# A long convolution and an MLP on one core: where the stores of batch 0's second stage are issued

## The chip, the cores and the metric

The kernel runs on one core of one Trainium2 chip. The metric is the device time of one execution in microseconds (us); what is compared is the median of several executions. The engines go by short names: PE is TensorE (PEld its weight loads), ACT is ScalarE, DVE is VectorE, POOL is GpSimd and SP is SyncE, which does no arithmetic and issues DMAs. All DMAs of the core are carried out by the same 16 DMA engines.

## The reference

A long convolution over 12480 positions is computed for two batches by Fourier transforms, multiplied by its input, and sent through an MLP. Cut to what matters (all arrays are float32):

```python
h_filt = (np.maximum(pos_emb @ w1, 0.0) @ w2) * window        # the filter
u = x * v                                                     # (2, 12480, 128)
Uf = np.fft.rfft(u, n=L, axis=1)                              # L = 2 * 12480
Hf = np.fft.rfft(h_filt, n=L, axis=0)
y = np.fft.irfft(Uf * Hf[None, :, :], n=L, axis=1)[:, :S, :]
attn = x * y
h = attn.reshape(B * S, D) @ w_in                             # 128 -> 2048
out = np.maximum(0.01 * h, h) @ w_out                         # 2048 -> 128
```

## The kernel before, in words

The transform of length 98 x 128 is done in steps of matrix products, with scratch arrays in DRAM between the steps. In time the kernel has three parts.

*First stage (to about 150 us).* The first transform step for batch 0 and for the filter. SP alone issues every DMA, loads and stores, among them the stores of the result `o` to the scratch array `scr1`.

*Second stage of batch 0 (about 150 to 320 us).* This is what the change touches. The work is cut into 25 chunks (`NCH`), taken in the order `ORD`, which begins with the chunks 13 to 24 and ends with 10 and 11. The loop `for i, c in enumerate(ORD)` runs over them. For each chunk

- `load_b` (line 705) brings a tile `bin`, 768 KB, from `scr1`; it is issued three chunks ahead, and there are four such tiles;
- `hidden` (line 790) puts the filter's part of the *next* chunk through PE (`ep`), and ACT copies it to `es` (line 793);
- PE makes the filter spectrum `hp` (line 846), ACT copies it to `hs` (line 850, two tiles `hs`), and `store_h` stores it to `hspec` with two DMAs of 256 KB (line 815): batch 1 reads it much later;
- PE makes the spectrum `up` (line 135); DVE and POOL multiply it by `hs` (`product`, lines 143 and 144) into `pin`; `up` has only one pair of PSUM tiles, so PE starts the next chunk's `up` when DVE has read this one;
- PE transforms back (`back_halves`, line 163, `dp`) the chunk *before*; `evac` copies it with ACT to `ct` (line 238, two tiles `ct`), and `store_back` stores it to `scr2` with one DMA of 512 KB (line 220);
- between these, a generator `weights` is advanced five steps a chunk. It loads a piece of the MLP's weights (lines 717 and 718, 256 KB each, every third chunk, eight pieces in all), and DVE, ACT and PE turn it into two parts each (lines 80 to 91, 732 to 762).

Late in the loop SP also begins the loads that the third part needs: `upper_c` and `rows_c` read `scr2` into `cin` (lines 629 to 650), `fetch_a` brings some 1.4 MB for batch 1 (lines 249, 67 and 69, twice), `load_gx` more (lines 609 to 620), and for the last two chunks `last_c` copies a few rows from `ct` straight into `cin` (line 657). The first MLP tile waits for the last of these.

*The MLP (from about 325 us to the end)* runs on PE, and batch 1's convolution is worked in between.

The order of the work is written out by hand: each engine takes its instructions in the order of the program, and one that waits holds all behind it on its engine. For DMAs this goes for the queue of the engine that issues them. In this stage the loads are issued by SP, and the stores of `hs` and of `ct` by ACT, between its copies. Each DMA also takes one of eight completion semaphores in turn (`DMAHW0` to `DMAHW7` in the rows below), which SP and ACT share; before it is issued it waits until the DMA that had that semaphore before has landed.

The kernel before has a list `late` in this loop that is always empty; a `flush` that empties it is called in the third part only.

Of the kernel before, what the change touches and what calls it, by code (L numbers as in the profile page):

```python
# [30 lines left out]
def tile_conv_mlp(ctx, tc, x, v, pos_emb, w1, w2, w_in, w_out, cf, cr, cg, cb, ci, cw, out):  # L31
    nc = tc.nc
# [77 lines left out]
    def run(g):  # L110
        for _ in g:
            pass
# [14 lines left out]
    def chunk(c):  # L127
        k0 = c * KC
        return k0, min(KC, NA - k0)
# [88 lines left out]
    def store_back(b, c, ct, eng):  # L218
        k0, n = chunk(c)
        eng.dma_start(out=scr2[b][k0:k0 + n].rearrange("k r m e -> (r m) k e"),  # L220
                          in_=ct[:, :n].rearrange("p k s d -> p k (s d)"))
# [13 lines left out]
    def back_evac(dp, ct, n):  # L235

        for s in range(2):
            nc.scalar.copy(ct[:, :n, s, :], dp[s][:, :n * D].rearrange("p (k d) -> p k d", d=D))
            yield


    with tc.manual_schedule():
# [17 lines left out]
        def mult_a(c):  # L260
            ft, (xt, vt) = got.pop(c)
            nc.gpsimd.tensor_tensor(out=xt, in0=xt, in1=vt, op=ALU.mult)
            u1[c] = ft, xt

        with ExitStack() as st:
# [89 lines left out]
            late = []  # L355
            for c in range(NC0):
# [23 lines left out]
                late = []  # L380
# [224 lines left out]
        def load_gx(t):  # L605
            b, mp = divmod(t, NT)
            g = gring()
            for r in range(2):
                nc.sync.dma_start(out=g[KH * r:KH * r + KH, :4 * NA],
                                  in_=cg[:KH, mp, r].rearrange("k p m a -> k (p m a)"))  # L610
            xt = xring()
            ms = slice(2 * mp, 2 * mp + 2)
            full = x[b, :(NA - 2) * NB, :].rearrange("(i w p n) d -> w i p n d", w=2, p=2, n=HB)
            for w in range(2):
                nc.sync.dma_start(out=xt[64 * w:64 * w + KH - 1], in_=full[w, :, :, ms, :])
            r0 = (NA - 2) * NB
            nc.sync.dma_start(out=xt[KH - 1:KH],
                              in_=x[b, r0:r0 + NB, :].rearrange("(o p n) d -> o p n d", o=1, p=2)[:, :, ms, :])
            r0 += NB + 2 * mp
            nc.sync.dma_start(out=xt[GAP - 1:GAP, 0], in_=x[b, None, r0:r0 + 2, :])  # L620
            ld[t] = (g, xt)
# [21 lines left out]
        def rows_c(t, j, lo, hi):  # L643

            b, mp = divmod(t, NT)
            ci_t = cin[t]
            ms = slice(2 * mp, 2 * mp + 2)
            ks = slice(KH * j + lo, KH * j + hi)
            for r in range(2):
                nc.sync.dma_start(out=ci_t[KH * r + lo:KH * r + hi, j].rearrange("k m s d -> k (m s d)"),  # L650
                                  in_=scr2[b][ks, r, ms, :].rearrange("k m e -> k (m e)"))

        def last_c(ct, k0, n, engs):

            for m in range(2):
                for r in range(2):
                    engs[2 * m + r].dma_start(out=cin[0][KH * r + k0:KH * r + k0 + n, 0, m],
                                      in_=ct[HB * r + m:HB * r + m + 1, :n])
# [38 lines left out]
        with ExitStack() as st:  # L697
# [4 lines left out]
            def load_b(c):  # L702
                k0, n = chunk(c)
                t = sbb.tile([128, KC, 2, C0], F32, tag="bin", name="bin", bufs=4)
                nc.sync.dma_start(out=t[:, :n].rearrange("p k s e -> p k (s e)"), in_=scr1[:, k0:k0 + n, :])
                bins[c] = t
# [61 lines left out]
            late = []  # L768
            turn = [0]

            def two(tag):
                return [psb.tile([128, 512], F32, tag=tag, name=tag + "p", bufs=2) for _ in range(2)]
# [6 lines left out]
            def ahead(n):  # L779
                for _ in range(4 * n):  # L780
                    next(conv)

            def hidden(c):

                n, t = chunk(c)[1], bins[c]
                ep = psb.tile([128, 2, 2, 2, 64], F32, tag="e", name="ep")
                for s in range(2):
                    for k in range(n):
                        i = 64 * (k % 2)
                        nc.tensor.matmul(ep[i:i + 64, k // 2, :, s, :], t[:, k, s, :FO], mb[:, s],  # L790
                                         start=True, stop=True)
                eh[c] = sbb.tile([128, 2, 2, 128], F32, tag="es", name="es")
                nc.scalar.copy(eh[c][:, :n // 2], ep[:, :n // 2].rearrange("p j r s q -> p j r (s q)"))

            def evac(c):
                ct = sbb.tile([128, KC, 2, D], F32, tag="ct", name="ct", bufs=2)
                k0, n = chunk(c)
                end = c == ORD[-1]
                dp = dps.pop(c)
                if end:  # L800
                    for s, copy in ((0, nc.scalar.copy), (1, nc.vector.tensor_copy)):
                        copy(ct[:, :n, s, :], dp[s][:, :n * D].rearrange("p (k d) -> p k d", d=D))
                else:
                    run(back_evac(dp, ct, n))
                if c in ORD[-2:]:
                    last_c(ct, k0, n, [nc.sync] * 3 + [nc.scalar if end else nc.sync])
                store_back(0, c, ct, nc.sync if end else nc.scalar)

            def store_h(c, hs, i):

                w = chunk(c)[1] * D

                def put(eng):
                    for s in range(2):
                        eng.dma_start(out=hspec[c][:, :, s, :w], in_=hs[HB * s:HB * s + HB, :, :w])
                put(nc.scalar)

            eh, dps = {}, {}
            first_c = upper_c(0)
# [1 line left out]
            next(conv)  # L821
            hidden(ORD[0])
            for i, c in enumerate(ORD):
                if i + 3 < NCH:
                    load_b(ORD[i + 3])
                if NCH - 10 <= i < NCH - 5:
                    next(first_c)
                if i == NCH - 2:
                    load_gx(0)
                if i == NCH - 1:  # L830
                    load_gx(1)
                    rows_c(0, 0, 0, (MID - 2) * KC)
                if i in FETCH:
                    fetch_a(FETCH.index(i))
                if i == NCH - 2:
                    mult_a(0)
                for f in late:
                    f()
                late = []
                n = chunk(c)[1]  # L840
                t, es = bins.pop(c), eh.pop(c)
                hp = two("h")
                for ri in range(2):
                    for k in range(n):
                        h, j = 64 * (k % 2), ri * n // 2 + k // 2
                        nc.tensor.matmul(hp[k % 2][:, D * j:D * j + D], es[h:h + 64, k // 2, ri, :], w22[h:h + 64, :],
                                         start=True, stop=True)
                hs = sbb.tile([128, 2, KC // 2, 2, D], F32, tag="hs", name="hs", bufs=2)
                for k in range(2):
                    nc.scalar.copy(hs[:, :, :n // 2, k, :],  # L850
                                   hp[k][:, :n * D].rearrange("p (r j d) -> p r j d", r=2, d=D))
                hs = hs.rearrange("p r j i d -> p r (j i d)")
                up = two("u")
                fwd(up, lambda s: t[:, :n, s, FO:], n)
                if i + 1 < NCH:
                    hidden(ORD[i + 1])
                store_h(c, hs, i)
                for _ in range(3):
                    next(wprep, None)
                pins[c] = sbb.tile([128, 2, 512], F32, tag="pin", name="pin", bufs=2)  # L860
                ab = [sbb.tile([128, 2, 512], F32, tag=g, name=g) for g in ("ta", "tb")]
                product(ab, up, hs, n * D, pins[c], nc.vector if i >= NCH - 2 else nc.gpsimd)
                if i >= 1:
                    b4 = ORD[i - 1]
                    dps[b4] = two("d")
                    back_halves(dps[b4], pins.pop(b4), b4)
                    evac(b4)
                for _ in range(2):
                    next(wprep, None)

            def flush():
                for f in late:
                    f()
                late.clear()

            ahead(1)
            run(wprep)
            mult_a(1)
            dps[ORD[-1]] = two("d")
            back_halves(dps[ORD[-1]], pins.pop(ORD[-1]), ORD[-1])  # L880
            evac(ORD[-1])
            run(join_hi(0))
            run(upper_c(1))
# [433 lines left out]
```

## Time and profile before

| | us |
|---|---|
| median of 3 executions | 1598.55 (1595.64 to 1606.63) |
| the profiled execution, its own time | 1601.6 |
| its span in the trace | 1599.7 |
| PE busy in the span | 1555.3 (97%) |
| DVE busy | 1138.7 (71%) |
| ACT busy | 998.1 (62%) |

The profile is of one execution. Its span runs from the first to the last instruction; the 1.9 us between span and time lie around it. Times in the rows below count from the span's start. A DMA-issuing instruction (engine names with a q: SPq, ACTq) is not counted as busy time of its engine, though it takes that engine's turn.

### The profile page before, as it was taken

To read this page: it belongs to the slowest core of one execution; us is meant where nothing else is said; L and a number is where in the kernel's file an instruction comes from. 1 tells how busy PE (TensorE), PEld (TensorE's weight loads), DVE (VectorE), ACT (ScalarE), POOL (GpSimd) and SP (SyncE) were. 2 spreads that over 40 slices of the span, in tenths; PEclk is the share of its full clock that TensorE was granted. 3 is DMA by queue.
4 is the path that set the end of the run, shared out by engine and by line. 5 is a ranking of instruction groups with operands and counts; after the bars stand their busy time and mean duration, and the time that the engine had idled before them with its cause. 6 is when DMAs were issued, how large, how long until landed. Compare 5 with 4: busy or idle time off the path is not lost.

```text
span 1599.7 us, 27485 instructions
## 1 busy us (share of the span) xinstructions
PE 1555.3 (97%) x9241; PEld 1322.6 (83%) x9241; DVE 1138.7 (71%) x1785; ACT 998.1 (62%) x2108; POOL 767.0 (48%) x806
## 2 busy tenths in 40 slices
PE   7888999899999999999999999999999999999998
PEld 7887555588889888888888888988888888888888
DVE  6874888756975566666676765677777777777776
ACT  2332555346664477777777776667777676777776
POOL 6772122146654275867776873633443433334310
PEclk9999999999999999999999999999999999999999
DMA  9998999767767477657556650421212212121200
GB/s 268 304 307 283 320 318 340 243 198 203 222 198 216 136 194 192 197 162 197 173 160 181 171 153 32 138 85 55 69 54 68 80 57 89 56 61 59 64 11 21
DMA packets 166268, 253.30 MB, mean 158 GB/s; under 512 B 14240, under 2 KB 118932, under 8 KB 163056
## 3 DMA queue, kind: packets, MB, share of 16 engines
q1 hardware_dynamic: 146388, 226.28, 47.7%
q10 hardware_dynamic: 19740, 25.28, 4.5%
q8 instruction: 73, 1.20, 0.3%
q14 instruction: 67, 0.55, 0.1%
HBM read 168.03 MB, written 83.43 MB: 157 GB/s over the span
## 4 chain that ended last, share of the span: by engine, by line
PE 75%; DMA 11%; DVE 8%; ACT 2%; issue 2%; POOL 1%; SPq 1%; ACTq 0%; DVEq 0%; POOLq 0%
PE mh L1009 29%; PE acc L1051 9%; PE acc L1052 9%; PE acc L1050 9%; PE yp L932 4%; PE cv L149 3%; DMA scr<-o 3%; PE cv L445 3%; DMA scr<-ct 2%; DMA ft<-in_cf_dram 2%; PE op L1082 2%; PE a L398 2%; PE zp L951 1%; PE up L135 1%; DVE ta L143 1%
## 5 line engine op out<-in xcount | busy, mean ns | idle before, releaser
L1014 DVE SCALAR_TENSOR_TENSOR rl<-mh,rh 128x512 fp32r<-128x512 f32 (+1 forms) x336 | 226.7, 682 | 198.7 <-ACT rh L1013 197.4
L1022 DVE TENSOR_TENSOR rl<-mh,rh 128x512 fp32r<-128x512 f32 (+2 forms) x416 | 277.4, 670 | 83.6 <-ACT rh L1021 75.1
L1017 ACT ACTIVATE mh<-mh 128x512 f32<-128x512 f32 (+2 forms) x416 | 236.9, 570 | 153.8 <-PE mh L1009 143.5
L1009 PE MATMUL mh<-zh,w_in_h 128*128 128x512 f32 (+3 forms) x800 | 315.9, 395 | 3.8 <-DVE rl L1014 2.6
L1009 PE MATMUL mh<-zl,w_in_h 128*128 128x512 f32 (+3 forms) x800 | 299.2, 374 | 0.3 <-POOL zl L965 0.2
L1051 PE MATMUL acc<-rl,w_out_h 128*128 128x512 f32 (+3 forms) x800 | 299.1, 374 | 0.1
L1050 PE MATMUL acc<-rh,w_out_h 128*128 128x512 f32 (+3 forms) x800 | 299.0, 374 | 0.0
L1052 PE MATMUL acc<-rh,w_out_l 128*128 128x512 f32 (+3 forms) x800 | 299.0, 374 | 0.0
L1009 PE MATMUL mh<-zh,w_in_l 128*128 128x512 f32 (+3 forms) x800 | 299.0, 374 | 0.0
L1013 ACT ACTIVATE rh<-mh 128x512 fp32r<-128x512 f32 (+1 forms) x336 | 199.1, 596 | 136.8 <-PE mh L1009 128.4
L965 POOL TENSOR_TENSOR zl<-zf,zh 128x390 fp32r<-128x390 f32 (+24 forms) x110 | 67.7, 628 | 395.7 <-ACT zh L964 371.0
L687 POOL TENSOR_TENSOR cp<-cq,cp 98x256 f32<-98x256 f32 x248 | 194.1, 783 | 29.3 <-DVE cp L675 12.6
L1019 DVE CAST rh<-mh 128x512 fp32r<-128x512 f32 (+2 forms) x208 | 139.5, 671 | 65.6 <-ACT mh L1017 65.3
L1009 PEld LDWEIGHTS mh<-zh,w_in_h 128*128 128x128 f32 x800 | 151.2, 189 | 30.1 <-DVE rl L1014 9.2
L1051 PEld LDWEIGHTS acc<-rl,w_out_h 128*128 128x128 f32 x800 | 151.2, 189 | 20.2 <-DVE rl L1022 0.4
L1050 PEld LDWEIGHTS acc<-rh,w_out_h 128*128 128x128 f32 x800 | 151.2, 189 | 19.8
L1052 PEld LDWEIGHTS acc<-rh,w_out_l 128*128 128x128 f32 x800 | 151.2, 189 | 19.7
L1009 PEld LDWEIGHTS mh<-zh,w_in_l 128*128 128x128 f32 x800 | 151.2, 189 | 19.7
L1009 PEld LDWEIGHTS mh<-zl,w_in_h 128*128 128x128 f32 x800 | 151.6, 190 | 15.9 <-POOL zl L965 0.6
L1021 ACT CAST rh<-mh 128x512 fp32r<-128x512 f32 (+2 forms) x208 | 118.7, 571 | 6.7
L684 POOL TENSOR_TENSOR cq<-cin 98x256 f32<-98x256 f32 x124 | 97.3, 784 | 0.9 <-DMA cin<-scr 0.8
L144 POOL TENSOR_TENSOR pin<-ta,tb 128x512 f32<-128x512 f32 (+1 forms) x23 | 28.8, 1253 | 130.7 <-DVE tb L143 130.7
(168 smaller groups left out, 2559.3 us busy)
## 6 DMA issues: line engine op xcount, KB each, us to landing
cin<-scr SPq DMA_DIRECT2D x318, 98.0 KB
hd<-hspec SPq DMA_DIRECT2D x48, 512.0 KB
bin<-scr SPq DMA_DIRECT2D x24, 768.0 KB
scr<-o SPq DMA_DIRECT2D x28, 588.0 KB
scr<-ct SPq DMA_DIRECT2D x25, 512.0 KB
scr1b<-o SPq DMA_DIRECT2D x32, 392.0 KB
hspec<-hs ACTq DMA_DIRECT2D x48, 256.0 KB
xm<-in_x_dram SPq DMA_DIRECT2D x128, 96.0 KB
```

The source lines that it names most:

```text
L684: eng.tensor_tensor(out=cq[:, p], in0=ci_t[:, 0, :, 0, :], in1=ci_t[:, 0, :, 1, :], op=op)
L687: eng.tensor_tensor(out=cp[:, p, w], in0=cq[:, p], in1=cp[:, p, 1], op=op)
L1009: nc.tensor.matmul(hp, u[:, fs], m, start=(i == 0), stop=(i == 2))
L1013: nc.scalar.activation(out=split2(rh), in_=plain(hp), func=AF.Relu)
L1014: nc.vector.scalar_tensor_tensor(out=split2(rl), in0=plain(hp), scalar=0.0, in1=split2(rh), op0=ALU.max, op1=ALU.subtract)
L1017: nc.scalar.activation(out=hp, in_=hp, func=AF.Lrelu, alpha=0.01)
L1019: nc.vector.tensor_copy(split2(rh), plain(hp))
L1021: nc.scalar.copy(split2(rh), plain(hp))
L1022: nc.vector.tensor_tensor(out=split2(rl), in0=plain(hp), in1=split2(rh), op=ALU.subtract)
L1050: nc.tensor.matmul(ap, w_out_h[:, f, :], rh, start=(f == 0 and not sums(k)), stop=False)
L1051: nc.tensor.matmul(ap, w_out_h[:, f, :], rl, start=False, stop=False)
L1052: nc.tensor.matmul(ap, w_out_l[:, f, :], rh, start=False, stop=(f == NF - 1))
```

## The change

Both kinds of store are taken from ACT's queue. `store_h` and `evac` no longer issue them but put them on the list `late`; the loop empties the list at the top of the next chunk, ahead of that chunk's `load_b`, and SP issues them there. A `flush` after the loop issues what the last chunk left. The last chunk's own `ct` store is issued by SP at once, as before. The one ACT copy of `last_c` (line 657) stays on ACT. Nothing else is changed: the same transfers of the same sizes, the same tiles, the same arithmetic.

```diff
@@ evac
-                store_back(0, c, ct, nc.sync if end else nc.scalar)
+                if end:
+                    store_back(0, c, ct, nc.sync)
+                else:
+                    late.append(lambda: store_back(0, c, ct, nc.sync))
@@ store_h
-                put(nc.scalar)
+                late.append(lambda: put(nc.sync))
@@ the loop over the chunks
             for i, c in enumerate(ORD):
+                for f in late:
+                    f()
+                late = []
                 if i + 3 < NCH:
                     load_b(ORD[i + 3])
...
-                for f in late:
-                    f()
-                late = []
@@ after the loop
+            flush()
             ahead(1)
             run(wprep)
```

On ACT, in the middle of the stage, one chunk before the change (`es`, `hs`, `ct` are the copies named above, `scr_0_63` is `scr2`):

```order
L850 COPY hs<-hp 128x4x128 x2
L793 COPY es<-ep 128x512
L815 DMA hspec<-hs 128x1x512 x2
L238 COPY ct<-dp 128x4x128 x2
L220 DMA scr_0_63<-ct 128x4x256
L742 COPY wts<-wt 128x256
L744 ACTIVATE wo_1895<-wo 128x256
```

Here the `hs` stores come after the `es` copy and the `ct` store after the `ct` copy. The same chunk now (line 853 is the old line 850):

```order
L853 COPY hs<-hp 128x4x128 x2
L793 COPY es<-ep 128x512
L238 COPY ct<-dp 128x4x128 x2
L742 COPY wts<-wt 128x256
L744 ACTIVATE wo_1892<-wo 128x256
```

The three DMA issues of a chunk are gone from between ACT's copies.

On SP, where the first `fetch_a` has just been issued (`ft` and `xv` are its tiles, `wi` and `wo` the last piece of the weights), before:

```order
L67 DMA xv_2651<-in_v_dram 1x2x512
L69 DMA xv_2651<-in_v_dram 1x2x512
L705 DMA bin<-scr_60 128x1536
L717 DMA wi_2755<-in_moe_w_in_dram 128x256
L718 DMA wo_2756<-in_moe_w_out_dram 128x2x128
L609 DMA gt<-in_cg_dram 49x392 x2
```

SP had only loads here. The same place now (line 818 is the old line 815):

```order
L67 DMA xv_2651<-in_v_dram 1x2x512
L69 DMA xv_2651<-in_v_dram 1x2x512
L818 DMA hspec<-hs 128x1x512 x2
L220 DMA scr_0_63<-ct 128x4x256
L705 DMA bin<-scr_60 128x1536
L717 DMA wi_2753<-in_moe_w_in_dram 128x256
L718 DMA wo_2754<-in_moe_w_out_dram 128x2x128
L818 DMA hspec<-hs 128x1x512 x2
L220 DMA scr_0_63<-ct 128x4x256
```

A chunk's two `hs` stores and the `ct` store now stand ahead of a `bin` load in one queue, and behind `fetch_a` where that was issued first.

On SP, at the stage's end, the difference:

```order
 L650 DMA cin<-scr_0_63 40x512 x2
-L657 DMA cin<-ct 4x1x256 x7
+L657 DMA cin<-ct 4x1x256 x4
+L818 DMA hspec<-hs 128x1x512 x2
+L220 DMA scr_0_63<-ct 128x4x256
+L657 DMA cin<-ct 4x1x256 x3
 L220 DMA scr_0_63<-ct 128x4x256
```

The seven small copies of `last_c` are now parted: 1 MB of stores stands between the four of chunk 10 and the three of chunk 11.

## Rows read from the trace of the kernel before

**Rows 1.** The page's head.
```profile
span 1599.7 us, 27485 instructions
```
**Rows 2.** Stretches: length, busy us (x instructions) by engine, PEclk, DMA share, GB/s.
```profile
148.00:154.00 6.00, 4.18 (x36) 3.07 (x38) 0.00 (x0) 1.66 (x3) 0.00 (x0) 0.77 0.96 381
160.00:260.00 100.00, 97.28 (x828) 57.88 (x826) 86.28 (x190) 51.16 (x104) 19.88 (x16) 1.00 0.97 322
260.00:280.00 20.00, 19.45 (x165) 11.19 (x163) 17.47 (x37) 9.67 (x20) 5.10 (x4) 1.00 1.01 345
280.00:300.00 20.00, 16.39 (x126) 9.07 (x124) 13.82 (x27) 8.24 (x17) 5.30 (x3) 0.91 0.91 277
300.00:320.00 20.00, 18.14 (x119) 11.92 (x116) 16.40 (x30) 6.97 (x14) 2.37 (x1) 1.00 0.67 208
```
**Rows 3.** PE's instructions in order of time: start, duration, what; each row one chunk's up.
```profile
182.19 1.94 PE L135 MATMUL up<-bin,mb 128*64 128x512 f32 x8
...
200.43 1.94 PE L135 MATMUL up<-bin,mb 128*64 128x512 f32 x8
...
260.72 1.94 PE L135 MATMUL up<-bin,mb 128*64 128x512 f32 x8 [0.21 <-DVE ta L143]
...
279.09 1.94 PE L135 MATMUL up<-bin,mb 128*64 128x512 f32 x8 [0.35 <-DVE ta L143]
...
304.22 1.94 PE L135 MATMUL up<-bin,mb 128*64 128x512 f32 x8 [1.59 <-DVE ta L143]
```
**Rows 4.** Waits of ACT by releaser, 160 to 260 us: total us, times, longest.
```profile
ACT ct L238 <- PE dp L163: 25.8, 17, 2.0
```
**Rows 5.** The tiles hs and ct: the stores that ACT issues, ns least/median/most.
```profile
L815 ACTq DMA_DIRECT2D hspec<-hs x50: 515/516/1186, 156.6 to 308.1; - x50
...
L220 ACTq DMA_DIRECT2D scr<-ct x24: 364/366/410, 164.1 to 310.1; - x24
```
**Rows 6.** DMA packets of 30:130, its SP queue (q1), then of 170:257 and 257:290.
```profile
DMA packets 21405, 30.59 MB, mean 306 GB/s; under 512 B 1287, under 2 KB 16506, under 8 KB 21396
...
q1 hardware_dynamic: 21396, 30.49, 93.0%
...
DMA packets 15817, 28.38 MB, mean 326 GB/s; under 512 B 1103, under 2 KB 9727, under 8 KB 15808
...
DMA packets 6096, 10.85 MB, mean 329 GB/s; under 512 B 435, under 2 KB 3577, under 8 KB 6093
```
**Rows 7.** ACT in order of time, with the idle time before and what ended it.
```profile
186.95 1.08 ACT L238 COPY ct<-dp 128x512 f32<-128x512 f32 x2 [1.32 <-PE dp L163]
...
275.45 3.18 ACTq L815 DMA_DIRECT2D hspec<-hs  x2
...
285.25 1.08 ACT L238 COPY ct<-dp 128x512 f32<-128x512 f32 x2 [0.83 <-PE dp L163]
291.19 0.37 ACTq L220 DMA_DIRECT2D scr<-ct  x1
...
299.71 4.16 ACTq L815 DMA_DIRECT2D hspec<-hs  x2
```
**Rows 8.** DVE in order of time, with the idle time before and what ended it.
```profile
282.99 0.43 DVE L747 TENSOR_TENSOR w_out_l<-wo,w_out_h 128x256 fp32r<-128x256 f32 x1 [2.69 <-ACT w_out_h L745]
...
288.76 0.29 DVE L80 TENSOR_SCALAR fa<-wi 128x256 uint32<-128x256 uint32 x1 [1.45 <-DMA wi<-in_moe_w_in_dram]
...
292.90 0.69 DVE L143 TENSOR_TENSOR ta<-up,hs 128x512 f32<-128x512 f32 x1 [1.14 <-ACT hs L850]
```
**Rows 9.** The chain that ended last, in order of time: start, us, what.
```profile
257.17 7.73 DMA hspec<-hs
...
281.40 8.61 DMA scr<-ct
...
315.81 1.68 DMA cin<-ct
```

**Rows 10.** SP in order of time: the small copies of last_c.
```profile
310.05 6.33 SPq L657 DMA_DIRECT2D cin<-ct  x7
```

## The prediction

> **What bounds the kernel now.** I read the page's head first, then the busy time by stretch, then each engine in order of time, and last the chain that ended last. The profiled execution took 1601.6 us with a span of 1599.7 [rows 1], so 1.9 us lie around it; it stands 3.05 us above the median of 1598.55. PE is busy 97% of the whole span (the table above) and is the bound after 325 us, where the change touches nothing, so what the second stage gains or loses goes through to the end one to one.
>
> The stage has two parts. From 160 to 260 us PE is busy 97.28 of 100 us and the DMA engines 97%, at 322 GB/s [rows 2]: two resources are nearly full at once, ACT is half idle. A full chunk takes a third of the way from 182.19 to 200.43, which is 6.08 us [rows 3]. From 260 us on the extra loads of the next stage come on top. The DMA share is 1.01 to 280, then falls to 0.91 and 0.67, while PE falls to 16.39 of 20 us [rows 2]. The six chunks from 260.72 to 304.22 take 43.50 us where six times 6.08 would be 36.48: **7.0 us are lost here**, of which only 0.1 before 279.09 (three chunks in 18.37 us) [rows 3].
>
> Where they go is seen on ACT and DVE. ACT issues two stores in 3.18 us at 275.45 and again in 4.16 at 299.71, where two take 1.03 (2 x 516 ns) by the median; the store at 291.19 follows a copy that had ended at 286.33, so ACT stood 4.86 us with the store at its head [rows 5, 7]. These issues wait for a completion semaphore, and ACT's copies stand behind them. DVE then waits 2.69 us for ACT's `w_out_h`, 1.45 for the last piece `wi` of the weights, which lands at about 288.7, and 1.14 for `hs` [rows 8].
>
> **The change part by part.** All bytes stay; 25 times two and 24 times one issue move from ACT to SP.
>
> *ACT's issue time* goes: 50 x 0.516 + 24 x 0.366 = 34.6 us over the stage [rows 5]. I cost this at nothing while PE and DMA are full. Over 160 to 260 us ACT waits 25.8 us for PE before its `ct` copies alone [rows 4]. If ACT's time did matter, the gain could be no more than what PE is idle there, 100 - 97.28 = 2.7 us.
>
> *The stores' start.* "A chunk late" is only so in the text of the program: SP comes early to the place and waits there for the copy. The `hs` store can start when `hs` is ready, one ACT copy earlier than before, and the `ct` store as before. A store of `hs` or `ct` must land before the tile is used again two chunks on, some 12 us; landing times in the chain are 7.73 and 8.61 us even where the DMA engines are full [rows 9]. That covers it, with 3 to 4 us to spare.
>
> *The loads* come later, since SP now waits for the `ct` copy first. In the chunk whose `up` runs from 182.19 to 184.13 the `ct` copy ends at 188.03 [rows 3, 7]: 3.9 us, and some 0.4 for the issue. A load is begun three chunks ahead, 18.2 us, and lands well within the rest, 14 us, while the queue before it holds a chunk's bytes (1.8 MB at 326 GB/s [rows 6], 5.6 us). Queued behind a load is the weights' piece and the next `hs` store; neither is late by this. Cost nothing in the steady part, as long as the one queue carries the bytes.
>
> *Does one queue carry them?* The trace has no loads and stores mixed on one queue in this stage. The nearest row is the first stage, where SP issued all: 306 GB/s at 93.0% of the engines' time, in packets of 30.59 MB / 21405 = 1.43 KB [rows 6]. The stage in question needs 326 GB/s from 170 to 257 us, in packets of 1.79 KB. By the one end nothing is lost: `bin` loads alone ran on that queue at 381 GB/s from 148 to 154 us [rows 2]. By the other the first stage's rate holds: 28.38 MB / 306 GB/s is 92.7 us where it was 87, so +5.7. Per unit of busy share the two are close: 306 / 0.93 = 329 against 322 / 0.97 = 332, 1% apart. I take +1.5, near the low end for that reason. The ends for the steady part are -2.7 and +5.7.
>
> The Trainium skill says, in "DMA: Bandwidth & Descriptors", section "Issuing engines are not separate DMA queues", that DMAs issued by several engines run on the same 16 engines and that spreading them only saves the sequencers' time. By that rule this term would be 0 instead of +1.5; the near equality of the two rates agrees, and no run of this kernel shows a single queue in this stage yet.
>
> *The last six chunks.* If ACT no longer holds, all of the 7.0 us could go; that is the far end. But the engines are full until 290: 10.85 MB in 33 us, 329 GB/s [rows 6], so what lands when is set by bytes. `wi` landed at 288.7 with a store of 512 KB, begun at 281.40, beside it until 290.0 [rows 9]. In one queue that store stands behind `wi`: 0.524 MB / 329 GB/s = 1.6 us earlier for `wi`. The 2.69 us of DVE before it are hidden then, since DVE comes earlier and waits for `wi` instead. Behind it the 1.14 us for `hs` go too. Against this the `hs` stores now stand behind `fetch_a` (1.4 MB) and the loads, and by the bytes ahead of it the second `hs` store from there lands some 0.7 us after its tile is wanted (an estimate, between 0 and the other end below). So -1.6 - 1.1 + 0.7 = -2.0. The other end is that chunks wait for all of `fetch_a` to pass: 1.4 MB / 329 GB/s = +4.3.
>
> *The stage's end.* The seven small copies are issued from 310.05 to 316.38 [rows 10], and the last, begun at 315.81, lands 1.68 us later, at 317.5 [rows 9]; the next stage's first sums wait for it. Now three issues (2 x 0.52 + 0.37 = 1.4 us [rows 5]) and 1.05 MB stand before chunk 11's three. At some 0.6 us each chunk 10's four are out by about 312.4 and chunk 11's three begin near 314.6, so the new issues fit between, with 0.8 us to spare. Their bytes take 1.05 MB / 329 GB/s = 3.2 us, begun from 312.4 to 313.8, of which about 1.0 may reach beyond the last copy's start. I take +1.0, with 0 and +3.2 as ends.
>
> *Sum*: +1.5 - 2.0 + 1.0 = +0.5 us. The profiled execution would come to 1602.1, the median to 1598.55 + 0.5, or **1599.0**. A measurement of this kernel can tell about 1%, 16 us, from no change, so this is no change.
>
> **The rivals.**
>
> *One queue carries less (slower).* The place is the whole stage, the price the first stage's 306 GB/s: +5.7 to 257 us, and 10.85 MB / 306 = 35.5 instead of 33, so +2.5, to 290; together +8, 1607. It decides as soon as one queue falls under the 326 GB/s needed. For it: the first stage on one queue never kept the engines over 93% on average. Against it: its packets are smaller, and the rates per share agree.
>
> *Stores behind loads (slower).* With two queues the stores went beside the loads: 7.73 us to land in full traffic [rows 9]. In one queue a store waits for all that is ahead, at the end for `fetch_a`; then the tail costs +4.3 instead of -2.0, the sum is +1.5 + 4.3 + 1.0 = +6.8, 1605. It decides where a landing passes 12 us, two chunks. For it: PE and DVE hang on two `hs` tiles. Against: the steady chunks have 3 to 4 us to spare. The Trainium skill, same page, section "Queues, rings and completion order", states that each DMA engine goes round between the queues that have work; by that rule ACT's stores had a share of their own that they lose now, and this rival is what it comes to. The trace agrees with such sharing but does not show the single queue.
>
> *ACT set free (faster).* All 7.0 us go and the end costs its 1.0: -6, 1592.5. For it: the issues on ACT of 3.18, 4.16 and the hold of 4.86 us. Against: the engines were full to 290 us whoever waited.
>
> **How the numbers follow.** Forecast, within 4 us: 0.52. One queue carries less: 0.24; stores behind loads: 0.12; ACT set free: 0.12. The range of 8 in 10 runs from 1591 (all of the tail's loss) to 1611 (the first rival at 1607 and the second's tail partly on top). Slower by over 1% needs more than 16 us: the first rival with both tails, 5.7 + 2.5 + 4.3 + 3.2 = 15.7, and a little more; 0.11 of the chances. Faster by over 1% is beyond any term here and is left 0.03 for what I do not see; the rest, 0.86, is within 1%.
>
> **What would show it.** In the profile after, ACT has no DMA issue of lines 815 and 220 in the stage, the `up` rows stay 6.08 us apart to about 279, DMA share 0.95 or more. Chunks of 6.3 us or more there, with DVE or PE waiting for `bin`, mean the first rival; ACT's `hs` and `ct` copies idle for a store, the second; the last `up` before 299, the third. The small copies of `last_c` should land within 1 us of 317.5 plus the stage's gain or loss. I am wrong altogether if the time after 325 us changes by itself.

## The result and the profile after

The changed kernel took **1620.19 us** by the median of 6 executions (1613.08 to 1622.28), the kernel before 1599.02 in its 6 beside them. The ratio is 1.0123, with an interval of 1.01 to 1.0147: slower by 1.2%, some 20 us (the ratios here and below are not the quotients of the two medians and differ from them by some 0.1% at most; the quotient here is 1.0132). The forecast of 1599.0 and its range to 1611 missed it. The profiled execution took 1619.26 us, and the head of its page shows a span 17.8 us longer than in [rows 1]:

```profile
span 1617.5 us, 27531 instructions
```

Busy time by stretch of the changed kernel (columns as in [rows 2]):

```profile
160.00:260.00 100.00, 93.47 (x794) 55.33 (x791) 82.90 (x181) 48.66 (x103) 19.90 (x16) 1.00 0.93 304
...
300.00:320.00 20.00, 15.92 (x87) 8.71 (x88) 19.52 (x33) 6.35 (x15) 6.38 (x3) 0.77 0.79 234
```

PE is down from 97.28 to 93.47 of 100 us in the steady part, DMA from 322 to 304 GB/s. That looks like the first rival, a queue that carries less; it is not, as shown below. DMA moves less because its issuer stands still.

Where in the stage the time is lost is read from the `up` rows of PE. After (first chunk, two neighbours, 21st, 24th and last chunk):

```profile
154.03 2.69 PE L135 MATMUL up<-bin,mb 128*64 128x512 f32 x8
...
177.26 1.94 PE L135 MATMUL up<-bin,mb 128*64 128x512 f32 x8
184.83 1.94 PE L135 MATMUL up<-bin,mb 128*64 128x512 f32 x8 [1.95 <-DVE ta L143]
...
278.11 1.94 PE L135 MATMUL up<-bin,mb 128*64 128x512 f32 x8 [0.73 <-DVE ta L143]
...
303.66 3.68 PE L135 MATMUL up<-bin,mb 128*64 128x512 f32 x8 [7.32 <-DVE ta L143]
312.94 1.94 PE L135 MATMUL up<-bin,mb 128*64 128x512 f32 x8 [0.42 <-DVE ta L143]
```

Before, the first and the 21st (the last is in [rows 3]):

```profile
152.79 2.83 PE L135 MATMUL up<-bin,mb 128*64 128x512 f32 x8
...
272.55 1.94 PE L135 MATMUL up<-bin,mb 128*64 128x512 f32 x8
```

From the first to the 21st chunk it was 119.8 us and is 124.1: **+4.3**. From there to the last, 31.7 and 34.8: **+3.2**. From the last `up` to DVE's first look at what the last small copy brought (`cq`, line 684), 13.6 and 19.8: **+6.2**. From there to the first MLP matmul +1.7, on which more below. With +1.2 in the stage's start (whose place moves between 149.7 and 157.2 us from profile to profile, whatever the kernel) and +1.2 in all the rest, that makes the 17.8.

What waits there, by DVE's waits from 145 to 345 us (total us, times, longest), after:

```profile
DVE fa L80 <- DMA wi<-in_moe_w_in_dram: 11.8, 6, 7.3
DVE cq L684 <- DMA cin<-ct: 9.0, 1, 9.0
```

and before:

```profile
DVE w_out_l L747 <- ACT w_out_h L745: 3.1, 2, 2.7
DVE cq L684 <- DMA cin<-ct: 2.6, 1, 2.6
DVE ta L143 <- ACT hs L850: 1.6, 2, 1.1
DVE fa L80 <- DMA wi<-in_moe_w_in_dram: 1.4, 1, 1.4
```

The waits for ACT (4.7 us, of [rows 8]) are gone, as the change would have it. In their place stands `wi`, the weights' piece, 10.4 us more, and the last small copy, 6.4 us more. The six waits for `wi` are one of 7.3 us in the last chunks and five of together 4.5 in the steady part, which is the +4.3.

Why `wi` is late is seen on SP. After:

```profile
190.73 0.37 SPq L220 DMA_DIRECT2D scr<-ct  x1
191.20 0.65 SPq L705 DMA_DIRECT2D bin<-scr  x1
191.95 0.74 SPq L717 DMA_DIRECT2D wi<-in_moe_w_in_dram  x1
...
286.54 3.19 SPq L818 DMA_DIRECT2D hspec<-hs  x2
290.34 0.38 SPq L220 DMA_DIRECT2D scr<-ct  x1
...
291.41 1.22 SPq L717 DMA_DIRECT2D wi<-in_moe_w_in_dram  x1
```

and the same two pieces before:

```profile
184.57 0.43 SPq L717 DMA_DIRECT2D wi<-in_moe_w_in_dram  x1
...
281.51 0.36 SPq L717 DMA_DIRECT2D wi<-in_moe_w_in_dram  x1
```

The piece is now issued 7.4 us later (6.1, less the later start), the last one 9.9; counted from the 21st `up`, which itself comes 5.6 us later, the last one is late by 4.3 (13.3 us behind that `up` instead of 9.0). Ahead of it in the queue stands the `ct` store, and SP stands there until ACT has copied `ct`. SP's waits from 160 to 260 us show it (ACT's lines 742 and 732 come directly behind its `ct` copy):

```profile
SPq L220 <- ACT wts L742: 19.4, 5, 4.9
SPq L220 <- ACT ct L238: 16.6, 6, 3.4
SPq L220 <- ACT w_in_h L732: 15.4, 5, 4.0
```

51 of the 100 us SP waits for ACT at one line. That by itself is no loss, since before it waited for PE with the `bin` loads, 74 of the 100 us; but `wi` is now behind a wait that ends later. DVE reaches `wi` in order; two of its rows after (start, us, and in brackets the idle time before):

```profile
198.82 0.29 DVE L80 TENSOR_SCALAR fa<-wi 128x256 uint32<-128x256 uint32 x1 [0.62 <-DMA wi<-in_moe_w_in_dram]
...
298.73 0.29 DVE L80 TENSOR_SCALAR fa<-wi 128x256 uint32<-128x256 uint32 x1 [7.25 <-DMA wi<-in_moe_w_in_dram]
```

and before, where the piece had been issued 10.9 us earlier and DVE did not wait:

```profile
195.50 0.28 DVE L80 TENSOR_SCALAR fa<-wi 128x256 uint32<-128x256 uint32 x1
```

The chain that ended last, traced back through this stage, now runs through the landing of `wi`, of these two pieces among others (start, us); before, none was among its longer pieces:

```profile
191.95 6.85 DMA wi<-in_moe_w_in_dram
...
291.41 7.30 DMA wi<-in_moe_w_in_dram
```

The stage's end on SP, after; in [rows 10] all seven copies took 6.33 us:

```profile
318.64 7.05 SPq L657 DMA_DIRECT2D cin<-ct  x4
325.73 1.22 SPq L818 DMA_DIRECT2D hspec<-hs  x2
327.00 0.69 SPq L220 DMA_DIRECT2D scr<-ct  x1
327.80 3.29 SPq L657 DMA_DIRECT2D cin<-ct  x3
```

and in the chain that ended last (start, us), ACT's one copy and SP's last:

```profile
323.26 1.84 DMA cin<-ct
...
330.52 1.92 DMA cin<-ct
```

Chunk 10's four copies take 7.05 us because the fourth is issued at 325.1, when the copy from 323.26 has landed. That one is ACT's, of chunk 11: it comes later in the work, but it has the turn before on the same completion semaphore. SP's waits from 300 to 335 us have it as

```profile
SPq L657 <- DMA cin<-ct: 4.5, 1, 4.5
```

Only then the two `hs` stores and the `ct` store follow, and behind them chunk 11's three copies.

### The profile page after: what moved, and what is told of

It reads as the page before. It is cut to its first block, busy times and chain, and to the rows that moved or that the text cites. A ratio compares the mean times of both kernels' runs of the same rounds, so it can differ in the third digit from the quotient of the medians.

```text
span 1617.5 us, 27531 instructions
## 1 busy us (share of the span) xinstructions
PE 1563.5 (97%) x9241; PEld 1330.8 (82%) x9241; DVE 1138.5 (70%) x1785; ACT 994.8 (62%) x2108; POOL 767.1 (47%) x806
## 4 chain that ended last, share of the span: by engine, by line
PE 73%; DMA 12%; DVE 7%; ACT 2%; issue 2%; POOL 2%; SPq 2%; DVEq 0%; ACTq 0%; POOLq 0%
PE mh L1013 28%; PE acc L1055 9%; PE acc L1056 9%; PE acc L1054 9%; PE yp L936 4%; PE cv L149 3%; PE cv L445 3%; DMA ft<-in_cf_dram 3%; DMA wi<-in_moe_w_in_dram 3%; DMA scr<-o 2%; PE op L1086 2%; PE zp L955 1%; DVE ta L143 1%; DMA vt<-in_v_dram 1%; PE up L135 1%
## 5 line engine op out<-in xcount | busy, mean ns | idle before, releaser
L687 POOL TENSOR_TENSOR cp<-cq,cp 98x256 f32<-98x256 f32 x248 | 194.0, 782 | 31.6 <-DVE cp L675 14.9
L1013 PEld LDWEIGHTS mh<-zh,w_in_l 128*128 128x128 f32 x800 | 151.7, 190 | 19.7
L1054 PEld LDWEIGHTS acc<-rh,w_out_h 128*128 128x128 f32 x800 | 151.2, 189 | 19.8
L1056 PEld LDWEIGHTS acc<-rh,w_out_l 128*128 128x128 f32 x800 | 151.2, 189 | 19.7
L144 POOL TENSOR_TENSOR pin<-ta,tb 128x512 f32<-128x512 f32 (+1 forms) x23 | 28.8, 1253 | 138.5 <-DVE tb L143 138.5
```

Source lines behind the costliest of these rows:

```text
L687: eng.tensor_tensor(out=cp[:, p, w], in0=cq[:, p], in1=cp[:, p, 1], op=op)
L1013: nc.tensor.matmul(hp, u[:, fs], m, start=(i == 0), stop=(i == 2))
L1054: nc.tensor.matmul(ap, w_out_h[:, f, :], rh, start=(f == 0 and not sums(k)), stop=False)
L1056: nc.tensor.matmul(ap, w_out_l[:, f, :], rh, start=False, stop=(f == NF - 1))
```

## Two theories and their rivals

**A, the weights' piece.** SP's wait for ACT's `ct` copy now stands ahead of `wi`, DVE stops for it, PE for DVE. Rival **B**: one queue carries fewer bytes. **C, the end.** A shared semaphore (C1) and three stores ahead of the last copies (C2) hold the copies on which the next stage waits. Rival to C: the last copies' own slowness.

All runs in one table. Ratio to the kernel before, in the profile first to 21st `up`, 21st to last, last `up` to `cq`, and DVE's wait for `wi`, in us:

| run | ratio (interval) | 1st-21st | 21st-last | last-`cq` | `wi` |
|---|---|---|---|---|---|
| before | 1 | 119.8 | 31.7 | 13.6 | 1.4 |
| after | 1.0123 (1.0100-1.0147) | 124.1 | 34.8 | 19.8 | 11.8 |
| e1 | 1.0048 (1.0031-1.0066) | 119.9 | 28.8 | 20.6 | 1.8 |
| e2 | 1.0182 (1.0149-1.0214) | 133.6 | 36.0 | 19.7 | 17.3 |
| e3 | 1.0088 (1.0060-1.0116) | 128.2 | 36.8 | 12.9 | 14.8 |
| e4 | 1.0132 (1.0111-1.0153) | 120.1 | 39.3 | 21.0 | 10.3 |
| e5 | 1.0076 (1.0056-1.0095) | 125.0 | 37.8 | 15.9 | 14.9 |
| e6 | 1.0005 (0.9990-1.0020) | 119.4 | 28.3 | 14.6 | 0 |
| e7 | 0.9992 (0.9978-1.0006) | 119.8 | 32.1 | 13.7 | 0.2 |
| e10 | 1.0019 (0.9999-1.0040) | 120.2 | 28.7 | 17.0 | 2.1 |
| e11 | 1.0079 (1.0050-1.0108) | 122.8 | 33.8 | 15.5 | 10.2 |
| e12 | 1.0070 (1.0047-1.0094) | 126.1 | 33.9 | 15.8 | 11.7 |
| e16 | 1.0082 (1.0050-1.0114) | 119.2 | 36.0 | 20.0 | 8.4 |
| e17 | 1.0047 (1.0030-1.0064) | 118.9 | 33.9 | 13.3 | 7.1 |

The times of the stretches come from one execution of each run, and that is not exact: the steady part of the changed kernel, which e3, e11 and e12 leave as it is, read 124.1, 128.2, 122.8 and 126.1. Where the cure is in, it is 118.9 to 120.2, so the two don't overlap. The last chunks and the end scatter likewise: the last chunks, which after, e11, e12, e16 and e17 have alike, read 33.8 to 36.0. The profiled execution also need not be a typical one: that of e6 took 1599.3 us where the median is 1603.3, that of e16 1619.79 where the median is 1614.83.

## Experiments on the weights' pieces

**e1, the weights early.** The changed kernel, with two buffers for the raw pieces and each loaded one piece sooner.

```diff
-wi64 = sbb.tile(..., bufs=1); wo64 = sbb.tile(..., bufs=1)
+wi64 = sbb.tile(..., bufs=2); wo64 = sbb.tile(..., bufs=2)
 load(0)
+load(1)
...
-if q + 1 < NQ: load(q + 1)
+if q + 2 < NQ: load(q + 2)
```

> The changed kernel, but the pieces of the MLP's weights are loaded one piece (three chunks) earlier, into two pairs of tiles instead of one. Theory A (the weights' piece wi now stands in SP's queue behind the ct store and a bin load, comes some 5 us later and DVE waits for it, 11.8 us in all): DVE's waits for wi fall under 1 us, the first to the 21st up take 120 us as in the kernel before and not 124, the last chunks lose some 3 us less, and the time falls by 5 to 9 us, to 1611 to 1615. Theory B (one queue carries fewer bytes): the first to the 21st up still take 123 to 125 us, 1618 to 1621.

Measured: 1608.46 us, ratio 1.0048, so 12 us of the 20 are gone, more than expected. The steady part is that of before. Its row of 160 to 260 us:

```profile
160.00:260.00 100.00, 96.08 (x816) 57.09 (x814) 86.92 (x191) 50.44 (x107) 21.17 (x17) 1.00 0.97 319
```

With every store on SP's queue the DMA engines are 97% busy at 319 GB/s, where [rows 2] had 97% at 322. B falls for the steady part: one queue carries it.

**e7, the same edit on the kernel before.**

> The kernel before with the weights' pieces alone two deep, as in e1. If e1's 11 us were only the mending of what the change had broken, the kernel before gains nothing from it, since its vector engine waits only 1.4 us for wi in the stage: 1597 to 1600 expected. Rival: the earlier pieces are a gain of their own (the 3.1 us that the vector engine waits for w_out_l, the last pieces of wi off the chain): 1590 to 1595.

Measured: 1599.92 us, 0.9992, no difference that can be told. So the earlier pieces are no gain of their own; in e1 they mend what the change broke.

**e16, the stores behind the weights.** No buffer is added. Except in the last five chunks the late stores are issued in the middle of the chunk, not at its top:

```diff
-                for f in late:
-                    f()
-                late = []
+                due, late = late, []
+                if i >= NCH - 5:
+                    for f in due:
+                        f()
+                    due = []
...
                 for _ in range(3):
                     next(wprep, None)
+                for f in due:
+                    f()
```

> The changed kernel with nothing deeper: in all chunks but the last five the late stores are issued in the middle of the chunk, behind its bin load and the weights' piece, by when ScalarE's ct copy that they wait for is long done. Theory A (the wait on ScalarE in front of wi is the loss in the steady part): first to 21st up 120 to 121.5 instead of 124.1, wi waits of that stretch under 2 us; the last five chunks and the end are as in the changed kernel, so time 1614 to 1617. Rival (the stores' bytes ahead of the weights matter, or any store on this queue): 123 us or more, time 1619 to 1621.

Measured: 1614.83 us, 1.0082. PE's first and 21st `up`, and DVE's wait for `wi`:

```profile
157.16 2.78 PE L135 MATMUL up<-bin,mb 128*64 128x512 f32 x8
...
276.40 1.94 PE L135 MATMUL up<-bin,mb 128*64 128x512 f32 x8
```
```profile
DVE fa L80 <- DMA wi<-in_moe_w_in_dram: 8.4, 1, 8.4
```

119.2 us with the same stores on the same queue, and of six waits for `wi` only the last chunks' one is left. The order in the queue is the whole loss of the steady part, and no buffer had to be added to take it back. This settles A there.

**e2, the stores in place.** SP issues each store where ACT did, not a chunk late: `put(nc.sync)` in `store_h`, `store_back(0, c, ct, nc.sync)` in `evac`.

> The changed kernel, but SP issues each store where it stands in the program, not a chunk late: the ct store now stands behind the weights' piece of its chunk and no longer ahead of it. One queue still carries all. Theory A: wi is loaded as early as in the kernel before in the steady part, the first to the 21st up take 120 to 121 us; the last piece is still late behind the first fetch, and the end is as in the changed kernel: 1613 to 1617. Theory B: nothing changes, 124 us and 1618 to 1621.

Measured: 1628.26 us, 1.0182, and the expectation missed: the steady part is 133.6 us, and DVE waits for `wi` 17.3 us in 8 times. SP now stands for the `ct` copy in the same chunk, so the piece behind it is later still. That the stores are a chunk late in the program is what kept the change's loss as small as it is.

**e4 and e5, each store alone.** e4 puts only the `hs` stores on SP (late), e5 only the `ct` stores.

```diff
# e4, evac
-                    late.append(lambda: store_back(0, c, ct, nc.sync))
+                    store_back(0, c, ct, nc.scalar)
# e5, store_h
-                late.append(lambda: put(nc.sync))
+                put(nc.scalar)
```

> Only the hs stores go to SP, a chunk late; the ct stores stay on ACT and in place. SP no longer waits for the ct copy ahead of the bin load and the weights. Theory A: DVE's waits for wi are as in the kernel before (1.4 us), the first to the 21st up take 120 us, 1599 to 1605. Theory B (SP's queue carries a quarter more bytes than before, but ACT's still half of the stores): 1605 to 1612.

> Only the ct stores on SyncE, a chunk late and ahead of the loads; the hs stores stay on ScalarE where they were. The other half of the run with the hs stores alone, whose steady part stayed at 120.1 us and whose last chunks and end lost. Theory A (SyncE's wait for ScalarE's ct copy is what holds the weights' pieces): the steady part's loss is the ct stores', first to 21st up 123 to 125 us with wi waits of 5 us or more. The two hs stores (512 KB) are then not in front of the last piece and the last copies: 21st to last up 31 to 34, last up to the last cin copy's landing 14 to 17; time 1606 to 1612. Rival (the hs stores' bytes and issue ahead of wi are what holds it, the ct store is innocent): first to 21st up 120 to 121, time 1600 to 1604.

Measured: e4 1621.54 us, 1.0132; e5 1615.26 us, 1.0076. The steady part came as expected: 120.1 us with the `hs` stores, 125.0 with the `ct` stores, so there the `ct` store's wait for ACT is the loss and the `hs` stores cost nothing. In the last chunks and in time both missed (e4 was to be at 1605 or less by A, e5 at 1612 or less): each kind alone costs more there than both together (39.3 and 37.8 us against 34.8, or 33.8 to 36.0 with the scatter). The rows of SP's waits from 276 to 312 us show what it stood for, in e4

```profile
SPq L815 <- DMA scr<-ct: 4.6, 1, 4.6
SPq L69 <- DMA scr<-ct: 3.7, 1, 3.7
```

and in e5

```profile
SPq L67 <- DMA hspec<-hs: 9.0, 1, 9.0
```

In both an instruction of SP waits for a store that *ACT* issues and with whose data it has nothing to do: the two share a completion semaphore. The last `wi` stands behind the 3.7 us in e4 and behind the 9.0 in e5; the 4.6 us come after `wi` was issued and hold an `hs` store. The kernel before has such waits too (`L69` for a `ct` store, also 3.7 us), so they do not tell by themselves how much is lost by them. In the changed kernel ACT issues none there, and SP waits for its own earlier DMAs instead, by the same view once for `bin`, 2.5 us, and twice for `fetch_a`'s `ft`, 3.8. The program's order of SP's instructions says which (number, line, DMA, what it waits for):

```
216 L705 DMA bin<-scr_60 128x1536 [waits DMAHW7_49,PE_49]
217 L249 DMA ft_2645<-in_cf_dram 98x1568 [waits DMAHW0_49]
...
224 L818 DMA hspec<-hs 128x1x512 [waits DMAHW7_49,Activation_49]
225 L818 DMA hspec<-hs 128x1x512 [waits DMAHW0_49]
...
228 L717 DMA wi_2753<-in_moe_w_in_dram 128x256 [waits DMAHW3_49,DVE_49]
```

Eight issues lie between a semaphore's two turns, so the `hs` store can't be issued before `bin` and `ft` have landed, and the last `wi` is behind that store. This is one way in which the last `wi` comes late, not the only one, as e3 below shows.

## Experiments on the stage's end

**e3, the last five chunks' stores back on ACT.**

```diff
# evac
+                elif ORD.index(c) >= NCH - 5 - 1:
+                    store_back(0, c, ct, nc.scalar)
# store_h
-                late.append(lambda: put(nc.sync))
+                if i >= NCH - 5:
+                    put(nc.scalar)
+                else:
+                    late.append(lambda: put(nc.sync))
```

> The changed kernel in the first twenty chunks; from the 21st on the stores are on ACT and in place, as before the change. What is lost up to the 21st up (4.3 us) stays by theory A and theory B alike. Theory C (half of the loss arises at the stage's end, where the small copies into cin wait for semaphores and stores in SP's queue): the last up to the landing of the last small copy takes 13 to 14 us again and not 19.5, the time falls to 1605 to 1611. If the loss were that of the whole stage on one queue, most of it would stay: 1615 or more.

Measured: 1613.84 us, 1.0088, 3 us above the expected times. Last `up` to `cq` is 12.9 us, and DVE's wait there 2.6 us, as before the change. So the end's loss is the stores' too. The last `wi` stays late here (9.2 us of wait): it is issued 14.3 us behind the 21st `up`, no sooner than with the change (13.3), although no `hs` or `ct` store of these chunks stands ahead of it on SP. SP's waits from 276 to 312 us have, ahead of it,

```profile
SPq L67 <- DMA hspec<-hs: 8.0, 2, 6.6
```

which are stores of ACT, waited for by the turn of the semaphores. With the stores on either queue the last `wi` is late, and with `wi` early the last chunks are short (e1, e6, e10: 28.3 to 28.8). A part of the delay is there before `fetch_a` begins: SP waits for an earlier `ct` copy ahead of it and starts it 0.9 us behind the 21st `up` here and 0.7 behind with the change, where it was 1.9 ahead of it before. How the rest divides between the place of the stores and the turn of the semaphores, the runs don't separate.

**e11, no copy on ACT.** The changed kernel with all four small copies of the last chunk on SP, so that nothing of ACT's stands in the turn of a semaphore.

```diff
-last_c(ct, k0, n, [nc.sync] * 3 + [nc.scalar if end else nc.sync])
+last_c(ct, k0, n, [nc.sync] * 4)
```

> The changed kernel with all four small cin copies of the last chunk on SyncE, none on ScalarE. Theory C1: chunk 10's fourth copy waited some 4.5 us on the completion count that it shares with ScalarE's later copy of chunk 11. Then this wait goes, the two hs stores and the ct store are issued some 4.5 us earlier, before the vector engine has chunk 11's ct ready, and the last copy lands some 4 us sooner: last up to landing 15 to 16 us instead of 19.5, the vector engine's cq wait 5 us or less, time 1614 to 1617. Theory C2: the 1 MB of stores in front of the last copies and their slow issue set the end, and the shared count costs nothing: 19 us or more, time 1619 to 1622.

Measured: 1612.45 us, 1.0079, better than expected, but with a wide spread: of its eight executions five took 1609 to 1615 us and three about 1620 or more. The profile is of one of the five (1609.9). SP in order of time:

```profile
311.92 2.57 SPq L657 DMA_DIRECT2D cin<-ct  x4
...
316.60 3.88 SPq L657 DMA_DIRECT2D cin<-ct  x4
```

Chunk 10's four copies take 2.57 us instead of 7.05. The 4.5 us were the shared semaphore, C1, and go with it: last `up` to `cq` 15.5.

**e12, the flush behind the last copies.** ACT keeps its copy; the call of `flush()` after the loop moves behind `evac(ORD[-1])`.

> The changed kernel with the last flush behind the last chunk's copies instead of ahead of them, ScalarE keeping its one copy. Theory C2 (the stores in front): the three copies follow the wait for the shared count at once, so the last lands some 2 us (the stores' issue) and some of the transfer time sooner: last up to landing 15 to 17 us, time 1615 to 1618. Theory C1 alone (the shared count is all): the landing stays within 1 us, 19 us, time 1619 to 1621.

Measured: 1614.28 us, 1.0070; last `up` to `cq` 15.8. The wait for the shared semaphore is still there, but the stores are not behind it. C1 alone takes back 4.3 us and C2 alone 4.0, of the 6.2 there are: whichever goes, a part of the other is covered. The rival, that the last copies are slow by themselves, has little room: the last chunk's three on SP are issued in 1.8 us without the stores ahead of them (1.8 before the change too) and in 3.3 behind them.

**e6, both places mended, the end on ACT** (e1 and e3 together).

> Theories A and C together: the loss has two places, the weights' pieces behind the stores in SP's queue, and the stage's end, and nothing else of size. This kernel mends the one as e1 did and the other as e3 did (the last five chunks' stores go back to ScalarE), while SyncE keeps the stores of all other chunks. Expected by A and C: first to 21st up some 120 us, 21st to last some 29 to 32, last up to the last cin copy's landing some 13; time 1596 to 1601. Rival B (SyncE's one queue carries less, so that a part of the loss stays whatever else is mended): first to 21st up 122 us or more, time 1604 or more.

Measured: 1603.3 us beside 1601.21 of before, 1.0005 (0.9990 to 1.0020). The 20 us are gone, 2 us short of the expected times by the median, with SyncE issuing four fifths of the stores. For B no remainder is left in the chunks whose stores SP issues that these executions could tell (0.2%, some 3 us, at most).

**e10, both mended on SyncE alone:** e1, e11 and e12 in one; ACT issues no store in the stage, as in the change.

> All stores of the stage stay on SyncE and ScalarE issues none, as in the changed kernel, with both places mended on SyncE itself: the weights' pieces two deep (as in e1), all four small cin copies of the last chunk on SyncE, and the last flush behind the last chunk's copies. Theories A and C (order in the queue, not the one queue, is the loss): first to 21st up 120, 21st to last 28 to 32, last up to landing 13 to 16, time 1598 to 1604, within 0.3% of before. Rival B at the end (one queue can't carry the last stores and copies as fast as two): landing 18 us or more behind the last up, time 1606 or more.

Measured: 1606.06 us beside 1601.63 of before, 2 us above the expected times and as much as the rival was to take; by the ratio 1.0019 (0.9999 to 1.0040), within the 0.3%. The end is 17.0 us, one more than expected and one less than the rival's. The two stretches together, from the 21st `up` to `cq`, are 45.7 us (before 45.3): the 3 us that the last chunks gain are lost again at the end. What comes last there is SP's issuing. ACT has chunk 10's `ct` copied at 308.90, but SP, which has issued one DMA after another since 300.63 (its waits from 300 to 320 us come to 1.5 us), reaches the copies 3.5 us later:

```profile
307.83 1.07 ACT L238 COPY ct<-dp 128x512 f32<-128x512 f32 x2 [6.52 <-PE dp L163]
```
```profile
312.44 5.11 SPq L657 DMA_DIRECT2D cin<-ct  x8
```

So at the end the time that SP takes to issue the stores and loads counts, once `wi` no longer covers it. Whether an issue is itself the limit or is held by full DMA engines is not shown, so B is not ruled out for this stretch.

**e17, e16 with the end mended on SyncE:** no buffer added.

> e16 with the end mended on SyncE as well (all four small copies of the last chunk there, the last flush behind them). A and C add: some 4 us less than e16 by the end, last up to landing 14 to 16 us, time 1609 to 1613; what is left over before is the last piece of wi behind fetch_a and the stores of the last five chunks (21st to last up 33 to 36 against 31.7). Rival (the two are the same time counted twice): 1614 or more.

Measured: 1609.41 us, 1.0047. A and C add. But the end is 13.3 us, as before the change, the first MLP matmul comes 1.5 us sooner than before, and yet the span is 5.0 us longer. The 6.5 us are lost behind it. The flush's 1 MB stands ahead of the next loads of `cin`, and POOL, which needs these, starts 3.1 us later than before, 4.6 counted from the first MLP matmul. Here, and before the change:

```profile
324.71 0.73 POOL L675 TENSOR_TENSOR cp<-cin 98x256 f32<-98x256 f32 x1 [18.01 <-DMA cin<-scr]
```
```profile
321.64 0.73 POOL L675 TENSOR_TENSOR cp<-cin 98x256 f32<-98x256 f32 x1 [14.83 <-PE yp L981]
```

From 320 to 340 us PE is busy 15.98 us at a mean clock of 0.83, where before it was 18.17 at 1.00. That the flush's place costs the 6.5 us is read from these rows; no run moves it alone.

No version beats the kernel before: the best, e6 and e7, are the same as it within what can be told.

## Why the prediction was wrong

*Steady part, "Queued behind a load is the weights' piece and the next `hs` store; neither is late by this. Cost nothing in the steady part".* This step failed, at +4.3 us. The prediction saw that SP's queue is delayed (4.3 us; `wi` measured 6.1) and set it against the 14 us of slack that a load has, three chunks ahead. It did not set it against the piece's own slack: issued 184.57, read 195.50, 10.9 us, of which landing takes most (6.85 for this piece in the chain after), so some 4 us to spare (an estimate, since the landing is that of the changed kernel) where 6 were taken. With a single buffer it is asked for only one piece ahead.

*"I take +1.5" for the one queue.* It measured 0.1 (e1: 119.9 against 119.8) and -0.6 in e16: nothing. (The 381 GB/s that stood for the low end, in [rows 2], are not of `bin` loads alone; a piece `wi` and `wo` is among them.) The Trainium skill, "DMA: Bandwidth & Descriptors", section "Issuing engines are not separate DMA queues", had 0 for this term, and the trace agrees with 0.97 at 319 GB/s.

*The last six chunks, "1.6 us earlier for `wi`", -2.0 in all.* This failed with its sign: the last piece is issued 4.3 us later by the 21st `up`, 9.9 by the clock of the trace, and 21st to last measured +3.2. The order was misread. The prediction put the `ct` store begun at 281.40 behind `wi` in the one queue; it is the stage's 20th, and the 20th is now the one at 290.34, ahead of `wi` at 291.41. The holds on ACT that the prediction found were real, and they went; DVE's waits for them are gone. But the two `hs` stores and that `ct` store now go ahead of `wi`, each with a completion to wait for. With `wi` early the same stretch is 28.8 us (e1) and 28.7 (e10), 3 below before, so that something like the -2.0 is there when `wi` doesn't take it; in e10 the end loses it again. What it comes from wasn't separated: e6, with these stores back on ACT, has 28.3, and e7 32.1. Nor was what makes the last `wi` late: in e3 it is as late with the stores on ACT.

*The stage's end, "so the new issues fit between, with 0.8 us to spare", +1.0.* Measured +6.2. The copies were taken at 0.6 us each, and that is what three of them take; the fourth waits 4.5 us for ACT's copy, and the stores stand behind that wait and not between. That the turn of the semaphores couples the two queues was in the text of the order, and was not followed.

*Right:* ACT's 34.6 us of issue cost nothing in the steady part (without them it is 119.2 us in e16, 119.8 before); the MLP changes little by itself (+1.2 us behind the first matmul). *The rivals:* the first, "one queue carries less", had the sign and 8 us, by a mechanism that e1 refutes; PE waits for `bin` no more than before (once, 2.2 us; before 2.0). The second had stores behind loads; it was loads behind stores. The third was right that the waits for ACT go, and wrong that nothing takes their place. A loss of over 1% had been given a chance of 0.11. And the times tell more than the 16 us that the prediction allowed: the interval of the ratio is 4 us to either side.

## What to carry to other kernels

When a store is moved to the queue that loads, look first at what the store waits for, then at every transfer behind it in the queue, and set the wait against the slack of the tightest of these: here a single-buffered piece of 256 KB, not the 768 KB loads. The remedy is the order (what nothing holds goes ahead of what waits) or one more buffer for the load that is tight; e16 and e1 each gave the steady part back whole. It gives back a loss and no more: nothing here is faster than the stores on ACT. And where two engines take completion semaphores in turn, moving one issue changes whom the next ones wait for: follow the turns at the places where the work is short of time.

## What the runs showed that was not expected

**The clock after an idle PE.** In the changed kernel PE waits for the last copies. By stretch (columns as in [rows 2]):

```profile
324.00:328.00 4.00, 3.15 (x29) 2.96 (x27) 0.00 (x0) 1.17 (x2) 0.00 (x0) 1.00 0.28 59
328.00:332.00 4.00, 0.00 (x0) 0.00 (x0) 0.00 (x0) 0.00 (x0) 0.00 (x0) 0.71 0.73 213
332.00:336.00 4.00, 2.25 (x12) 1.84 (x13) 2.84 (x7) 0.00 (x0) 0.00 (x0) 0.50 0.62 200
...
344.00:348.00 4.00, 3.81 (x25) 3.10 (x23) 3.90 (x10) 1.30 (x3) 0.00 (x0) 1.00 0.90 256
```

PE stands still, the granted clock goes to 0.50, which is 1.2 GHz, and has a mean of 1.00 again only in the row from 344 us. The first MLP matmul, after and before:

```profile
339.74 0.69 PE L1013 MATMUL mh<-zh,w_in_h 128*128 128x390 f32 x1 [0.70 <-ACT zh L1000]
```
```profile
323.10 0.43 PE L1009 MATMUL mh<-zh,w_in_h 128*128 128x390 f32 x1 [0.70 <-ACT zh L996]
```

From `cq` to this matmul it is 5.3 us in the kernel before, e3, e6, e7 and e17, whose ends are up to 14.6 us, and 7.0 in the changed kernel, e1, e2, e4 and e16, whose ends are 19.7 or more (6.0 to 7.0 in those between): the wait costs 1.7 us on top of itself. PE's rows between the two show it: eight `yp` matmuls take 1.12 us at 0.50 (L985) and 0.66 at 1.00 (L981).

**Half of the stores on each queue was worse than all on one.** With only one kind of store on SP the last chunks took 3 to 4.5 us longer than with both (2 to 5 with the scatter), though fewer bytes stand ahead of `wi` in SP's queue; the rows of e4 and e5 above show SP waiting for ACT's stores instead. That these waits are the cause is not shown by a run of its own.
